# Out-projection put in the plan six matmuls at a time, with a later hand-over to TensorE assumed and one whole-bank group a chunk

## The chip, the cores and the metric

The kernel runs on one core of a Trainium2 chip. Its time is the device time of one execution in microseconds, as the median of several runs. Engines are named as in the profile: PE is TensorE (PEld its weight loads), DVE is VectorE, ACT is ScalarE, POOL is GpSimd, SP the queue that issues the transfers.

## The reference

A gated scan over 6080 steps of 256 features, and behind it two feed-forward layers from 256 to 2048 and back, the first with a leaky ReLU, the second with an ELU:

```python
for t in range(S):
    h = f[:, t] * h + i[:, t] * x[:, t]
    y[:, t] = h
...
h = x @ w_in
g = np.maximum(0.01 * h, h)                                        # first layer
g = np.where(h > 0.0, h, alpha * (np.exp(np.minimum(h, 0.0)) - 1.0))   # second layer
return (g @ w_out)
```

All is float32.

## The kernel before, in words

**Tiles.** The steps are cut into 12 chunks: eleven of 512 and, as number 4, one of 448 (`sizes`). Features lie on partitions, steps along the columns. The 2048 hidden features are worked through in four groups q = 0 to 3 of 512. A float32 product is made of three matmuls (`mm3`, L605 to L607): each operand is split into a high part and a rest, and high x high, high x rest and rest x high are summed in a PSUM bank of 128 x 512. Where the moving operand has 512 columns, `mm3` cuts it into two halves of 256 and does three matmuls on each, unless its last argument `whole` is true; then it does three of 512 columns.

**One group of one chunk** (`group`, by layer l, chunk c and group q). The in-projection is done with seven products in place of eight (`product`, six matmuls of 256 columns each, three for either hidden half). They go to three banks: X, R and Y, where Y is the bank `seed`. Between them X is copied out four times by ScalarE: `z1` (L688) into Y, `z2` and `z4` (`snap`, L652) into SBUF. VectorE adds the bank R to z4 (`add`, L655), and only then may the next product on R run. So three chains go from TensorE to ScalarE or on to VectorE and back to TensorE inside each group: product X(S1,T1), snapshot z4, addition C22, product R(A22,T4); and product X(S1,T1), snapshot z4, product X(S4,B22); and the same with z2. Then come the activations (in layer two an exponential, L715 and L726, and VectorE's L717 and L728), a cast to the high part by ScalarE (L744, L838) and the rest by VectorE (L747, L841). These are the operands of the out-projection, which sums into two banks `yb[0]` and `yb[1]` over the four groups of a chunk. For two of the four groups the odd half of the out-projection is again done with seven products (`some`). All the rest is `straight` (L772): operations O0, O1, E0, E1 (odd or even half, j = 0 or 1), each with two outputs k, so twelve matmuls of 256 columns. In the last operation of a group, E1, `whole` is set for q < 2 in layer one and q < 3 in layer two, and it is then six matmuls of 512 columns; the text calls such six a whole group. The last chunk of layer two is done with operands swapped (L785 to L787). In the short chunk all matmuls of the out-projection have 448 columns and are never cut.

**The order.** Nothing is ordered at run time. The program first collects all operations with an engine, an estimated cost, what each follows, and which buffer it takes and gives back (`Plan.add`). `Plan.emit` then plays a list schedule through with these costs: for the engine that can start soonest it takes, among the operations that can start within 0.1 of the first, the one with the earliest rank, which is handed back from the due times of those that use its result. An operation's result counts as ready for a user at its end, plus `late` (0.1 for TensorE), plus `HOP`, 0.15. From TensorE to TensorE nothing is added. The order in which operations are taken is the order of the instructions on each engine; the chip then runs each engine's row in that order and waits with semaphores.

Of the kernel before, what the change touches and what calls it, by code (L numbers as in the profile page):

```python
# [16 lines left out]
P = 128  # L17
# [9 lines left out]
class Plan:  # L27
# [3 lines left out]


    HOP = 0.15

    def __init__(self, pools):
        self.pools = {name: [(0.0, i, t) for i, t in enumerate(tiles)] for name, tiles in pools.items()}
# [2 lines left out]
    def add(self, engine, cost, due, run, after=(), take=(), give=(), late=0.0):  # L39
# [4 lines left out]
        self.ops.append(op)  # L44
        return op

    def emit(self, near):
        free = {}
        open_ = {}
        for i, op in enumerate(self.ops):  # L50
            op.index = i
            op.missing = len(op.after)
            for a in op.after:
                a.users.append(op)
            if not op.missing:
                open_.setdefault(op.engine, []).append(op)
        for op in reversed(self.ops):
            for u in op.users:
                t = u.rank - op.cost - op.late - self.HOP
                op.rank = t if op.rank is None else min(t, op.rank)  # L60
        left = len(self.ops)
        while left:
            best = None
            for e, ops in open_.items():
                starts = []
                for op in ops:
                    t = max(free.get(e, 0.0), op.ready)
                    want = {}
                    for _, _, pool in op.take:
                        want[pool] = want.get(pool, 0) + 1  # L70
                    for pool, n in want.items():
                        have = self.pools[pool]
                        t = max(t, heapq.nsmallest(n, have)[-1][0]) if len(have) >= n else float("inf")
                    starts.append((t, op))
                if not starts:
                    continue
                first = min(t for t, _ in starts)
                if first == float("inf"):
                    continue
                t, op = min(((t, op) for t, op in starts if t <= first + near), key=lambda p: (p[1].rank, p[1].index))  # L80
                if best is None or t < best[0]:
                    best = (t, op)
            if not best:
                for o in [o for v in open_.values() for o in v][:40]:
                    print(o.engine, o.run, [(p, len(self.pools[p])) for _, _, p in o.take])
            assert best, "no operation can start"
            t, op = best
            for store, name, pool in op.take:
                store[name] = heapq.heappop(self.pools[pool])
            end = t + op.cost  # L90
            free[op.engine] = end
            done = end + op.late + self.HOP
            op.run()
            for store, name, pool in op.give:
                _, i, tl = store[name]
                heapq.heappush(self.pools[pool], (done, i, tl))
            open_[op.engine].remove(op)
            for u in op.users:
                u.missing -= 1
                u.ready = max(u.ready, end if u.engine == op.engine == "PE" else done)  # L100
                if not u.missing:
                    open_.setdefault(u.engine, []).append(u)
            left -= 1
# [3 lines left out]
def kernel(  # L107
# [27 lines left out]
    KD = D // P  # L135
# [116 lines left out]
    for l, c, q in stream:  # L252
        n = sizes[c]
# [169 lines left out]
    def wop(u, s):  # L423

        return tuple(w[u][:, j * size[u] + s * P : j * size[u] + (s + 1) * P] for j in (0, 1))
# [188 lines left out]
    def group(i):  # L614
        l, c, q = stream[i]
        n = sizes[c]
# [3 lines left out]
        b = {}  # L620
# [112 lines left out]
        def gate(name, j):  # L733
            return b[name][2][:, j * 2 * CH : j * 2 * CH + 2 * n]

        gates = {}
# [33 lines left out]
            prev[0] = o  # L770

        def straight(name, r, j):  # L772
            def run(fresh):
                hi, lo = (gate(name, s)[:, j * n : (j + 1) * n] for s in (0, 1))
                if not swapped:
                    for k in range(KD):
                        mm3(yb[k][2][:, :n], wop((r, q), 2 * j + k), (hi, lo), k in fresh, False,
                            (r, j) == ("E", 1) and q < (2 if l == 1 else 3))
                    return

                wh, wl = (w[r, q][:, z * size[r, q] + j * D : z * size[r, q] + (j + 1) * D] for z in (0, 1))
                for t in range(n // P):
                    dst = yb[t // 2][2][:, t % 2 * D : (t % 2 + 1) * D]
                    ah, al = (s[:, t * P : (t + 1) * P] for s in (hi, lo))
                    nc.tensor.matmul(dst, ah, wh, start=t // 2 in fresh and t % 2 == 0, stop=False, skip_group_check=True)  # L785
                    nc.tensor.matmul(dst, ah, wl, start=False, stop=False, skip_group_check=True)  # L786
                    nc.tensor.matmul(dst, al, wh, start=False, stop=False, skip_group_check=True)  # L787

            out_(3 * KD, run, (0, 1), [gates[name], *wo[r]], [(b, name, "op")] if j else [])


        C11, C12, C21, C22 = (1, 1), (1, 0), (0, 1), (0, 0)
# [213 lines left out]
```

## Time and profile before

| | |
|---|---|
| Median of 3 runs | 1012.66 us (1011.34 to 1013.00) |
| The profiled execution | 1012.59 us, of which 1010.8 are its span |
| Mean granted clock of TensorE | 0.999 of full |
| VectorE, ScalarE busy | 883.9 us (87%), 775.4 us (77%) |
| The chain that ended last | 92% of the span on TensorE, 4% on VectorE, 2% on ScalarE |

The page gives the busy time of each engine and where the chain runs that ended last. A matmul is recorded as longer than the distance to the next one, since they overlap; how fast the stream goes is read from the starts in the timeline, with the number of rows between two of them.

### The profile page before, as it was taken

What the parts mean: (1) busy time and instruction counts of PE and PEld (TensorE: products, weight loads), DVE (VectorE), ACT (ScalarE), POOL (GpSimd) and SP (SyncE); (2) the same over time, 40 slices, a digit from 0 to 9 for tenths busy, and PEclk for the clock granted to TensorE, in tenths of its full rate; (3) what the DMA queues carried; (4) which work ended last, traced back from release to release, by engine and by line L of the source; (5) the groups of instructions that cost most, each with busy time, mean ns of one, the idle gap of its engine ahead of it and who ended that gap; (6) DMA issues with size and microseconds to landing.
All of it is one profiled execution on the core that took longest, in us unless ns stands there. A gap on an engine that the chain in (4) does not pass through costs nothing.

```text
span 1010.8 us, 19956 instructions
## 1 busy us (share of the span) xinstructions
PE 996.8 (99%) x8152; PEld 977.3 (97%) x8152; DVE 883.9 (87%) x1352; ACT 775.4 (77%) x1135; POOL 32.0 (3%) x38
## 2 busy tenths in 40 slices
PE   7999999999999999999999999999999999999998
PEld 6999999999999999999999999999999999999997
DVE  6899979999999999876688998998989989889875
ACT  6777777788887978876778877787877777877764
POOL 1120000011010000000000000000000000000000
PEclk9999999999999999999999999999999999999999
DMA  6542304345255443303840111101101021010110
GB/s 187 136 118 51 79 11 95 108 120 152 89 137 147 114 121 114 82 22 115 298 162 21 22 30 32 22 21 43 19 22 21 23 43 21 22 22 23 32 21 22
DMA packets 159083, 74.34 MB, mean 74 GB/s; under 512 B 132496, under 2 KB 146832, under 8 KB 158992
## 3 DMA queue, kind: packets, MB, share of 16 engines
q1 hardware_dynamic: 158992, 73.08, 27.0%
q8 instruction: 63, 1.03, 0.4%
q14 instruction: 28, 0.23, 0.1%
HBM read 48.01 MB, written 25.03 MB: 72 GB/s over the span
## 4 chain that ended last, share of the span: by engine, by line
PE 92%; DVE 4%; ACT 2%; DMA 1%; issue 1%; SPq 0%; DVEq 0%
PE bank L607 28%; PE bank L606 28%; PE bank L605 28%; PE seed L607 2%; PE seed L605 2%; PE seed L606 2%; DVE op L747 1%; PE bank L787 1%; DMA raw<-in_f_logit_dram 1%; PE bank L785 0%; ACT op L744 0%; PE bank L786 0%; DVE h L826 0%; DVE ws L717 0%; DVE op L841 0%
## 5 line engine op out<-in xcount | busy, mean ns | idle before, releaser
L605 PE MATMUL bank<-op,wI 128*128 128x256 f32 (+1 forms) x1152 | 321.5, 279 | 0.5 <-ACT sn L652 0.5
L607 PE MATMUL bank<-op,wI 128*128 128x256 f32 (+1 forms) x1152 | 320.7, 278 | 0.6 <-DVE wI L386 0.6
L606 PE MATMUL bank<-op,wI 128*128 128x256 f32 (+1 forms) x1152 | 320.7, 278 | 0.0
L606 PEld LDWEIGHTS bank<-op,wI 128*128 128x128 f32 x1152 | 218.6, 190 | 2.8 <-DVE op L492 0.2
L605 PEld LDWEIGHTS bank<-op,wI 128*128 128x128 f32 x1152 | 217.3, 189 | 3.6 <-ACT sn L652 0.7
L607 PEld LDWEIGHTS bank<-op,wI 128*128 128x128 f32 x1152 | 217.3, 189 | 0.9 <-DVE wI L386 0.9
L606 PE MATMUL bank<-op,wO 128*128 128x256 f32 (+2 forms) x680 | 190.6, 280 | 1.9 <-DVE op L747 1.6
L605 PE MATMUL bank<-op,wO 128*128 128x256 f32 (+2 forms) x680 | 190.4, 280 | 0.0
L607 PE MATMUL bank<-op,wO 128*128 128x256 f32 (+2 forms) x680 | 190.3, 280 | 0.0
L606 PE MATMUL bank<-op,wE 128*128 128x256 f32 (+2 forms) x600 | 182.0, 303 | 0.2 <-DVE op L747 0.2
L607 PE MATMUL bank<-op,wE 128*128 128x256 f32 (+2 forms) x600 | 181.8, 303 | 0.0
L605 PE MATMUL bank<-op,wE 128*128 128x256 f32 (+2 forms) x600 | 181.8, 303 | 0.0
L655 DVE TENSOR_TENSOR h<-bank,sn 128x512 f32<-128x512 f32 (+1 forms) x176 | 119.4, 678 | 26.4 <-ACT sn L652 13.9
L652 ACT COPY sn<-bank 128x512 f32<-128x512 f32 (+1 forms) x176 | 102.2, 580 | 43.0 <-PE bank L607 40.9
L606 PEld LDWEIGHTS bank<-op,wO 128*128 128x128 f32 x680 | 128.7, 189 | 2.5 <-DVE op L747 1.8
L607 PEld LDWEIGHTS bank<-op,wO 128*128 128x128 f32 x680 | 127.9, 188 | 0.2
L605 PEld LDWEIGHTS bank<-op,wO 128*128 128x128 f32 x680 | 127.8, 188 | 0.2
L607 PEld LDWEIGHTS bank<-op,wE 128*128 128x128 f32 x600 | 112.8, 188 | 4.9
L606 PEld LDWEIGHTS bank<-op,wE 128*128 128x128 f32 x600 | 113.5, 189 | 3.0 <-DVE op L747 0.4
L605 PEld LDWEIGHTS bank<-op,wE 128*128 128x128 f32 x600 | 112.8, 188 | 2.6
L747 DVE TENSOR_TENSOR op<-h,op 128x1024 fp32r<-128x1024 f32 (+1 forms) x78 | 96.5, 1237 | 17.8 <-ACT op L744 17.4
L747 DVE TENSOR_TENSOR op<-ws,op 128x1024 fp32r<-128x1024 f32 (+1 forms) x74 | 89.4, 1211 | 15.9 <-ACT op L744 15.9
(109 smaller groups left out, 1821.2 us busy)
## 6 DMA issues: line engine op xcount, KB each, us to landing
ws<-in_moe_w_in_dram SPq DMA_DIRECT2D x32, 255.6 KB, 3.6
ws<-in_moe_w_out_dram SPq DMA_DIRECT2D x32, 255.6 KB, 3.2
w2dI<-ws SPq DMA_DIRECT2D x16, 448.0 KB, 3.3
wI<-w2dI SPq DMA_DIRECT2D x8, 896.0 KB, 6.6
y1d<-t SPq DMA_DIRECT2D x22, 256.0 KB, 2.1
bt<-y1d SPq DMA_DIRECT2D x22, 256.0 KB, 2.8
out_dram<-t SPq DMA_DIRECT2D x80, 64.0 KB, 2.0
raw<-in_f_logit_dram SPq DMA_DIRECT2D x72, 64.0 KB, 3.3
```

The costliest lines, as they stand in the source:

```text
L605: nc.tensor.matmul(ps[:, s], wop[0], a[0][:, s], start=start and z == 0, stop=False, skip_group_check=True)
L606: nc.tensor.matmul(ps[:, s], wop[0], a[1][:, s], start=False, stop=False, skip_group_check=True)
L607: nc.tensor.matmul(ps[:, s], wop[1], a[0][:, s], start=False, stop=stop, skip_group_check=True)
L652: return act(s1(2 * h), None, lambda: nc.scalar.copy(out=ps(name), in_=ps("X")), after, take=[(b, name, "sn")])
L655: return dve(v1(2 * h), None, lambda: nc.vector.tensor_tensor(out=half(name, s), in0=two(ps(bank)), in1=two(ps(sn)), op=ALU.add), after, **k)
L747: gates[name] = dve(v1(2 * n), None, lambda name=name, g=g: nc.vector.tensor_tensor(out=gate(name, 1), in0=whole(g), in1=gate(name, 0).bit ...
L787: nc.tensor.matmul(dst, al, wh, start=False, stop=False, skip_group_check=True)
```

## The change

Three things are changed. A result of VectorE or ScalarE counts as ready for TensorE 0.35 after its end, 0.15 as before for any other user (`hop`, used in the ranks and in the readiness). The operations of `straight` are put into the plan one output k at a time, six matmuls each, so that other work may stand between them and each output bank is done for itself. And `whole` is left only in E1 of q = 0, which alone stays one operation over both outputs; E1 of q = 1, and of q = 2 in layer two, is now cut into halves.

```diff
+    SPARE = 0.2
...
+    def hop(self, op, user=None):
+        spare = op.engine in ("DVE", "ACT") and (user is None or user.engine == "PE")
+        return self.HOP + (self.SPARE if spare else 0.0)
...
-                t = u.rank - op.cost - op.late - self.HOP
+                t = u.rank - op.cost - op.late - self.hop(op, u)
...
+            later = end + op.late + self.hop(op)
...
-                u.ready = max(u.ready, end if u.engine == op.engine == "PE" else done)
+                u.ready = max(u.ready, end if u.engine == op.engine == "PE" else later if u.engine == "PE" else done)
...
         def straight(name, r, j):
+            def ops(s):
+                return gate(name, s)[:, j * n : (j + 1) * n]
+
+            unbroken = (r, j) == ("E", 1) and q < 1
+
+            def some_of(*ks):
+                def run(fresh):
+                    for k in ks:
+                        mm3(yb[k][2][:, :n], wop((r, q), 2 * j + k), (ops(0), ops(1)), k in fresh, False, unbroken)
+
+                return run
+
             def run(fresh):
-                hi, lo = (gate(name, s)[:, j * n : (j + 1) * n] for s in (0, 1))
-                if not swapped:
-                    for k in range(KD):
-                        mm3(yb[k][2][:, :n], wop((r, q), 2 * j + k), (hi, lo), k in fresh, False,
-                            (r, j) == ("E", 1) and q < (2 if l == 1 else 3))
-                    return
...
-            out_(3 * KD, run, (0, 1), [gates[name], *wo[r]], [(b, name, "op")] if j else [])
+            if swapped:
+                out_(3 * KD, run, (0, 1), [gates[name], *wo[r]], [(b, name, "op")] if j else [])
+                return
+            for ks in [tuple(range(KD))] if unbroken else [(k,) for k in range(KD)]:
+                out_(3 * len(ks), some_of(*ks), ks, [gates[name], *wo[r]], [(b, name, "op")] if j and ks[-1] == KD - 1 else [])
```

Line numbers of the changed kernel are higher: L605 to L607 become L611 to L613, L652 L658, L655 L661, L717 L723, L728 L734, L744 L750, L747 L753.

**VectorE, layer two, chunk 1, q = 3.** The last rows up to and around the addition that the product R(A22,T4) waits for (L655, now L661; `bt` and `op` with L455 or L461 are the operands of a later chunk). Before:

```order
L747 TENSOR_TENSOR op_128<-ws_135,op_128 128x1024
L455 TENSOR_TENSOR op_126<-bt_129,op_126 128x768
L728 SCALAR_TENSOR_TENSOR ws_136<-ws_136,h_130 128x1024
L455 TENSOR_TENSOR op_125<-bt_129,op_125 128x768
L747 TENSOR_TENSOR op_127<-ws_136,op_127 128x1024
L455 TENSOR_TENSOR op_125<-bt_129,op_125 128x256
L655 TENSOR_TENSOR h_132<-bank_116,sn_138 128x2x256
```

Now:

```order
L753 TENSOR_TENSOR op_122<-ws_134,op_122 128x1024
L461 TENSOR_TENSOR op_125<-bt_129,op_125 128x768
L461 TENSOR_TENSOR op_123<-bt_129,op_123 128x768
L734 SCALAR_TENSOR_TENSOR ws_135<-ws_135,h_132 128x1024
L661 TENSOR_TENSOR h_133<-bank_119,sn_138 128x2x256
L461 TENSOR_TENSOR op_123<-bt_129,op_123 128x256
L753 TENSOR_TENSOR op_126<-ws_135,op_126 128x1024
```

The small L455 and the wide L747 ahead of the addition have moved behind it, and L734, the counterpart of L728, stands directly in front.

**TensorE, layer two, chunk 1, E1 of q = 1.** `wE_74` is the weight of this operation. Before, and the first matmul of what follows:

```order
L605 MATMUL bank_115<-op_127,wE_74 128x512
L606 MATMUL bank_115<-op_127,wE_74 128x512
L607 MATMUL bank_115<-op_127,wE_74 128x512
L605 MATMUL bank_121<-op_127,wE_74 128x512
L606 MATMUL bank_121<-op_127,wE_74 128x512
L607 MATMUL bank_121<-op_127,wE_74 128x512
L605 MATMUL bank_120<-op_123,wI_69 128x256
```

Now:

```order
L611 MATMUL bank_118<-op_126,wE_74 128x256
L612 MATMUL bank_118<-op_126,wE_74 128x256
L613 MATMUL bank_118<-op_126,wE_74 128x256
L611 MATMUL bank_118<-op_126,wE_74 128x256
L612 MATMUL bank_118<-op_126,wE_74 128x256
L613 MATMUL bank_118<-op_126,wE_74 128x256
L611 MATMUL bank_116<-op_127,wI_69 128x256
```

The whole group has become two operations of six halves, and the first matmul of a product (`wI`) follows behind the one; the other six stand twelve rows further on.

**ScalarE, layer one, chunk 2, q = 2.** From the snapshot z1 (L688, now L694) over z2 to z4 (both L652, now L658). Before:

```order
L688 COPY seed_114<-bank_116 128x512
L299 CAST wI_69<-h_133 128x384
L299 CAST wI_70<-h_131 128x384
L299 CAST wI_69<-h_133 128x128
L652 COPY sn_137<-bank_116 128x512
L299 CAST wI_70<-h_131 128x128
L701 ACTIVATE h_132<-seed_114 128x2x256
L652 COPY sn_138<-bank_116 128x512
```

Now:

```order
L694 COPY seed_114<-bank_116 128x512
L712 ACTIVATE h_131<-h_131 128x1024
L658 COPY sn_137<-bank_116 128x512
L305 CAST wI_69<-h_133 128x384
L305 CAST wI_70<-h_130 128x384
L305 CAST wI_69<-h_133 128x128
L305 CAST wI_70<-h_130 128x128
L750 CAST op_124<-h_131 128x1024
L658 COPY sn_138<-bank_116 128x512
```

All four casts of weights (L305) and the wide cast of an operand (L750) now stand between z2 and z4; before, three of the four and the wide one stood ahead of z2. In TensorE's row, six matmuls now stand between the product that z4 copies and the next on that bank, where it was twelve.

## Rows read from the trace of the kernel before

**Rows 1.** The page, section 1 (engines) and the granted clock in 40 slices.

```profile
PE 996.8 (99%) x8152; PEld 977.3 (97%) x8152; DVE 883.9 (87%) x1352; ACT 775.4 (77%) x1135; POOL 32.0 (3%) x38
...
PEclk9999999999999999999999999999999999999999
```

**Rows 2.** TensorE's timeline from 374 us: start us, us, engine line op.

```profile
373.89 0.28 PE L605 MATMUL bank<-op,wI 128*128 128x256 f32 x1
...
395.99 0.28 PE L605 MATMUL seed<-op,wI 128*128 128x256 f32 x1
```

**Rows 3.** Timeline of TensorE, 753 to 768 us, first and last row.

```profile
752.80 0.28 PE L605 MATMUL bank<-op,wO 128*128 128x256 f32 x1
...
768.00 0.28 PE L605 MATMUL bank<-op,wE 128*128 128x256 f32 x1
```

**Rows 4.** Windows of TensorE: us, busy (matmuls), clock, DMA share, GB/s.

```profile
299.00:325.00 26.00, 26.00 (x222) 1.00 0.37 109
582.00:667.00 85.00, 85.00 (x689) 1.00 0.14 31
746.00:973.00 227.00, 227.00 (x1837) 1.00 0.12 25
```

**Rows 5.** TensorE's timeline at 560 us, a wait in q=1.

```profile
560.39 0.31 PE L605 MATMUL bank<-op,wI 128*128 128x256 f32 x1
560.53 0.28 PE L606 MATMUL bank<-op,wI 128*128 128x256 f32 x1
560.65 0.28 PE L607 MATMUL bank<-op,wI 128*128 128x256 f32 x1
```

**Rows 6.** TensorE's timeline at 745 us, a wait in q=3.

```profile
745.68 0.35 PE L605 MATMUL bank<-op,wI 128*128 128x256 f32 x1
745.88 0.28 PE L606 MATMUL bank<-op,wI 128*128 128x256 f32 x1
```

**Rows 7.** Timeline of TensorE, 524 to 526 us, around a whole group.

```profile
524.63 0.40 PE L605 MATMUL bank<-op,wE 128*128 128x512 f32 x1
...
526.03 0.28 PE L605 MATMUL bank<-op,wI 128*128 128x256 f32 x1
...
526.38 0.28 PE L605 MATMUL bank<-op,wI 128*128 128x256 f32 x1
```

**Rows 8.** Timeline of TensorE, 750 to 752 us, around another whole group.

```profile
750.70 0.39 PE L605 MATMUL bank<-op,wE 128*128 128x512 f32 x1
...
752.10 0.28 PE L605 MATMUL bank<-op,wI 128*128 128x256 f32 x1
```

**Rows 9.** Groups by form: whole-bank matmuls of one line (others alike).

```profile
L606 PE MATMUL bank<-op,wE 128*128 128x512 f32 x104 | 41.1, 395 | 0.0
```

**Rows 10.** VectorE's timeline, 743 to 746 us, before that wait.

```profile
743.44 1.22 DVE L747 TENSOR_TENSOR op<-ws,op 128x1024 fp32r<-128x1024 f32 x1 [0.63 <-ACT op L744]
744.58 0.42 DVE L455 TENSOR_TENSOR op<-bt,op 128x256 fp32r<-128x256 f32 x1
744.92 0.68 DVE L655 TENSOR_TENSOR h<-bank,sn 128x512 f32<-128x512 f32 x1
```

**Rows 11.** VectorE's timeline, 552 to 560 us, before a wait in q=1.

```profile
552.45 0.69 DVE L717 SCALAR_TENSOR_TENSOR ws<-ws,seed 128x512 f32<-128x512 f32 x1 [0.35 <-ACT ws L715]
...
559.58 0.68 DVE L655 TENSOR_TENSOR h<-bank,sn 128x512 f32<-128x512 f32 x1
```

**Rows 12.** Timeline of TensorE, 719 to 725 us, the entry to chunk 5.

```profile
720.79 0.38 PE L605 MATMUL bank<-op,wI 128*128 128x256 f32 x1 [0.52 <-ACT sn L652]
```

**Rows 13.** ScalarE groups by form: busy us, mean ns, idle before.

```profile
L652 ACT COPY sn<-bank 128x512 f32<-128x512 f32 x160 | 93.7, 585 | 39.8 <-PE bank L607 38.0
...
L299 ACT CAST wI<-h 128x384 fp32r<-128x384 f32 x8 | 3.8, 509 | 1.8 <-DVE h L273 1.8
...
L299 ACT CAST wI<-h 128x128 fp32r<-128x128 f32 x8 | 2.2, 297 | 0.4 <-DVE h L273 0.4
...
L744 ACT CAST op<-h 128x1024 fp32r<-128x1024 f32 x72 | 75.6, 1050 | 0.9
```

More of the change, by code (lines that the diff above doesn't have):

```diff
@@ L783, in run @@
                     dst = yb[t // 2][2][:, t % 2 * D : (t % 2 + 1) * D]
-                    ah, al = (s[:, t * P : (t + 1) * P] for s in (hi, lo))
+                    ah, al = (ops(s)[:, t * P : (t + 1) * P] for s in (0, 1))
                     nc.tensor.matmul(dst, ah, wh, start=t // 2 in fresh and t % 2 == 0, stop=False, skip_group_check=True)
```

## The prediction

> **What bounds the kernel now.** I read the page first: TensorE is busy for 99% of the span, at full clock in all forty slices, 2.4 GHz, so a busy share says nothing more [rows 1]. What is left to see is how far apart its matmuls start, and that is in the timeline of TensorE alone. Between 373.89 and 395.99 us, 195 steps of 256 columns take 22.10 us: 113.3 ns each [rows 2]. Between 752.80 and 768.00 us, 129 steps of the same size take 15.20 us: 117.8 ns [rows 3]. The stream has two paces, 4.5 ns apart, and the granted clock is 1.00 in the slow stretches too, so the clock is not what separates them [rows 4].
>
> What changes the pace is seen next. At 560.39 and at 745.68 us a product on bank R, which must wait for VectorE's addition (L655), starts its second matmul 0.14 and 0.20 us later instead of 0.113, and the steps behind it are 0.12 [rows 5, 6]. A wait of 0.03 to 0.08 us thus costs little itself, but leaves the stream slow. At 524.63 a group of six whole-bank matmuls comes by, and behind it the steps are 0.113 again [rows 7]; at 750.70 another comes by and the stream stays slow [rows 8, 3]. Following every wait over 0.03 us through the timeline, I count 14 stretches behind one: 6 were fast at once, 6 slow until the next whole group, 2 slow until something large broke them (582 to 667 and 746 to 973 us). These two hold most of the loss.
>
> **The change, part by part.** The sum is made against the profiled execution, 1012.59 us, which is the median of the runs shown (1012.66) less 0.07.
>
> *The long slow stretches.* Both begin at the same place, the addition in group q = 3 of a layer-two chunk. VectorE idles 0.63 us for ScalarE's cast, does L747 and a small L455, then the addition, 744.92 to 745.60, and the matmul that needs it stands at 745.68 [rows 6, 10]. In the changed order L747 and that L455 stand behind the addition, and L734 (L728 of before) stands in front. Counting from the start of product X(S1,T1): the snapshot of X ends at 1.57, since ScalarE comes to it 0.1 late; L734 waits for an exponential that ends at 0.58, and ends at 1.83; the addition then runs from 1.76 to 2.44 (durations and overlaps as in [rows 10]). The product on R stands 24 matmuls from that start, as before, 24 x 0.1133 = 2.72. That leaves 0.28 us, where before 0.08 was left between its end and the matmul's late start. I take the wait as gone in all ten full chunks. In the two windows there are 689 + 1837 = 2526 matmuls, 132 of them whole, so some 2390 at 4.5 ns, 10.7 us [rows 4]. The third wait of this kind, at 541 us, cost 42 steps, 0.2 us, and the waits themselves 3 x 0.08. Together **-11.1 us**; 0 if the wait stays.
>
> *The wait in q = 1 of layer two.* Here nothing is won: from L717, which waits for an exponential, VectorE works without a break up to the addition, 552.45 to 559.58 [rows 11], and both orders put the same VectorE work and the same 87 matmuls between the product that starts this chain and the one that ends it. Before, this wait came in three chunks only, since a slow stream has no need to wait; with a fast one it comes in each of ten. It costs 0.035 us [rows 5] and 30 slow steps up to the chunk's whole group, 0.14: seven more, **+1.2 us**. Ends: -0.5 (none left) and the price of staying slow, a rival below.
>
> *Whole banks.* 104 x 3 = 312 whole matmuls are 52 groups of six [rows 9]; one a full chunk leaves 21, so 31 go. Six whole ones take 1.40 us, 233 ns each, fast or slow [rows 7, 8]; two halves at the fast pace take 226.7. So 31 x 6 x 6.7 ns = **-1.2 us**; at the slow pace two halves take 235.6, which would make it +0.4. The Trainium skill (TensorE: Matmul & The Clock Gate, "Wait — 56ns, not 53.3ns?") has each matmul cost its columns at 2.4 GHz and a fixed 2.5 ns more. By it 186 more matmuls would cost +0.5 us, and the sum would be 1.7 us higher; the rows measure the wide one as the dearer.
>
> *The entry to chunk 5 of layer two.* After the short chunk TensorE stands idle 0.52 us for a snapshot [rows 12], and twice more before 724 us. Split operations put 77.25 matmuls (of 256 columns) over this chain instead of 72: 5.25 x 0.1133 = **-0.6 us** (0 to -1.2, if the waits behind it shrink as much again).
>
> *New waits in layer one.* The new order takes cover away in two places. In chunk 2, q = 2, product X(S4,B22) now follows X(S1,T1) with 6 matmuls between, 12 before, and ScalarE has the four casts L305 and the wide L750 between the two snapshots. From the end of X(S2,T2) ScalarE needs 0.58 + 2 x 0.51 + 2 x 0.30 + 1.05 + 0.58 = 3.8 us [rows 13], less five overlaps of some 0.08 as in [rows 10], and 0.3 to start and to hand over; TensorE has 30 x 0.1133 = 3.4. A wait of 0.3 us follows, more if VectorE is late with what is cast. In chunk 7, q = 2, a wide cast moves in the same way between the snapshots: 0 to 0.6. Behind each the stream may be slow for some 325 steps, as the next whole group is a chunk away, 1.5 us. Against that, the slow steps from 299 to 325 us, 222 of them, 1.0 us [rows 4], may or may not come back. I take 0.6 for the waits and 1.4 for the pace, **+2.0 us** (-1.0 to +3.6).
>
> DMA issues, GpSimd and the operand stages move by a few places, and the list of TensorE's waits has none on a load after the first 20 us: at nothing, since the loads land long before their use; a load that came late would show as a wait of TensorE in tenths. The last chunk keeps its operations whole and its order: nothing.
>
> Sum: 1012.6 - 11.1 + 1.2 - 1.2 - 0.6 + 2.0 = **1002.9 us**.
>
> **The rivals.** (1) *One stretch stays slow.* Of 14 waits, 2 left a pace that whole groups did not break. If the wait at chunk 5 does so, layer two stays slow from 724 to 973 us, some 2130 steps, 9.6 us, less six waits of q = 1: 1011.5. If the one at chunk 7 of layer one does, 323 to 667 us are slow, 13.1 us less 2.2: 1013.8. For it: there is no later wait to shake it loose. Against: 12 of 14. (2) *The wait in q = 3 stays*, because ScalarE reaches the snapshot 0.3 us later than I worked out: then the long stretches come as before, 1012.6 - 1.2 - 0.6 + 2.0 = 1012.8. For it: ScalarE works without a break there. The change would then do nothing that it says. (3) *Slower.* The one mechanism: with 31 whole groups gone and the small waits too, nothing breaks a slow pace once it has come. If the stream turns slow for good at chunk 7 of layer one, and again behind the short chunk, 323 to 973 us are slow: 1002.9 + 10.9 + 8.6 = 1022.4. It decides at the first whole group behind 323 us: if the steps behind it are 0.118, this is the case. For it is that the whole group at 750.70 broke nothing [rows 8]; against it, the groups at 34, 325, 524, 546, 564 and 727 us did. (4) *Better.* No new wait and none in q = 1: 998.
>
> **How the numbers follow.** A measurement of this kernel tells 0.2%, 2 us, from no change: faster is below 1010.6, slower above 1014.7. I give my forecast 0.66 (998 to 1008), the better case 0.04, one slow stretch 0.12, the wait in q = 3 0.08, slow for good 0.10. The first two are faster, 0.70; the next two are the same, 0.20; the last slower, 0.10. The range goes from the better case, 998, to 1012.5, which takes in about half of the two middle cases.
>
> **What would show it.** Right: steps of 0.113 us in 582 to 667 and 746 to 973 us, no wait at the addition of q = 3, and a short slow stretch of 30 steps in q = 1 of each layer-two chunk. The whole groups number 21. New waits near 127 and 323 us. Wrong: steps of 0.118 over tens of microseconds behind any wait; or a wait of over 0.03 us at the addition of q = 3, where L734 would end later than 1.83 us behind the product's start.

## The result, and the profile after

| | before | after |
|---|---|---|
| Median (lowest to highest, runs) | 1021.49 us (1011.34 to 1024.93, 19) | 1006.29 us (999.79 to 1011.36, 19) |
| The profiled execution, its span | 1012.59 us, 1010.8 | 1008.28 us, 1006.3 |

The ratio of the times is 0.9894, 95% interval 0.9869 to 0.9919: faster by 1.1%; the two medians alone lie 1.5% apart. (Ratios here leave out runs more than 1.5% above the fastest of their kernel.) Both kernels spread by over ten microseconds from one execution to the next, and the three runs of before that were shown ahead of the prediction were at the low end. The two profiled executions are therefore only 4.3 us apart, and none of the slower executions of before has a profile: what its median of 1021.49 consists of is not shown. The changed kernel was profiled twice more, among the experiments, at 1002.53 and 1001.90 us.

The page of after, engines and granted clock, against [rows 1]:

```profile
PE 992.5 (99%) x8338; PEld 980.5 (97%) x8338; DVE 876.7 (87%) x1352; ACT 773.5 (77%) x1135; POOL 37.1 (4%) x38
...
PEclk9999999999999999999999999999999999999999
```

TensorE is still the bound, at the same clock. The timeline of TensorE, first and last row of a stretch behind 733 us and of one behind 569 us:

```profile
733.24 0.28 PE L611 MATMUL seed<-op,wI 128*128 128x256 f32 x1
...
755.00 0.28 PE L611 MATMUL bank<-op,wE 128*128 128x256 f32 x1
...
569.82 0.28 PE L612 MATMUL bank<-op,wI 128*128 128x256 f32 x1
...
591.96 0.28 PE L611 MATMUL bank<-op,wE 128*128 128x256 f32 x1
```

The first has 192 steps in 21.76 us, 113.3 ns each; the second 188 in 22.14 us, 117.8 ns. The two paces of [rows 2, 3] are there unchanged; what changed is where they lie. From 746 to 973 us, slow before [rows 4], the stream is now fast; from 531 to 669 us it is slow. The windows view (us, busy and matmuls, clock, DMA share, GB/s) shows the same clock in both:

```profile
531.00:669.00 138.00, 138.00 (x1156) 1.00 0.11 24
733.00:968.00 235.00, 235.00 (x2042) 1.00 0.12 25
```

The addition of q = 3 in layer two, chunk 5, in VectorE's timeline, and the start of the next product in TensorE's, against [rows 6, 10]:

```profile
745.73 1.23 DVE L734 SCALAR_TENSOR_TENSOR ws<-ws,h 128x1024 f32<-128x1024 f32 x1
746.88 0.69 DVE L661 TENSOR_TENSOR h<-bank,sn 128x512 f32<-128x512 f32 x1
747.48 0.41 DVE L461 TENSOR_TENSOR op<-bt,op 128x256 fp32r<-128x256 f32 x1
...
747.86 0.28 PE L611 MATMUL bank<-op,wI 128*128 128x256 f32 x1
```

The addition ends at 747.57, 0.29 us ahead of that product; the wait is gone. The one in q = 1 is still there, at the same place of the chunk as in [rows 5]:

```profile
767.92 0.31 PE L611 MATMUL bank<-op,wI 128*128 128x256 f32 x1
768.06 0.28 PE L612 MATMUL bank<-op,wI 128*128 128x256 f32 x1
768.18 0.28 PE L613 MATMUL bank<-op,wI 128*128 128x256 f32 x1
```

It is 0.14 in place of 0.113 long, and the stream is fast again five steps behind it. The entry to chunk 5 and the two new waits of layer one, chunk 2 and chunk 7, each in q = 2:

```profile
727.50 0.39 PE L611 MATMUL bank<-op,wI 128*128 128x256 f32 x1 [0.23 <-DVE h L661]
...
130.71 0.38 PE L611 MATMUL bank<-op,wI 128*128 128x256 f32 x1
...
329.68 0.39 PE L611 MATMUL bank<-op,wI 128*128 128x256 f32 x1 [0.38 <-ACT sn L658]
```

And the groups by form, against [rows 9]: 42 whole matmuls a line, which is 21 groups of six.

```profile
L612 PE MATMUL bank<-op,wE 128*128 128x512 f32 x42 | 16.6, 395 | 0.0
```

**Where the time went.** Counting every step of TensorE from the starts in the two traces, where a step of 256 columns of 116 to 121 ns is a slow one and a longer one a step that waited: 3101 slow steps before, 2132 after, 13.6 and 9.3 us over the fast pace, so -4.3. Steps that waited, behind the first 25 us, cost 6.4 and 7.5 us, +1.0, and ahead of that +0.2. The whole matmuls cost 1.8 and 0.7 us more than halves, -1.1; what comes after the last matmul has started, -0.2. That is -4.4 of the 4.5 by which the spans differ. In the two later profiles of the changed kernel there are 1234 and 1055 slow steps. Their spans are 5.8 and 6.5 us shorter than that of the first, of which slow steps are 4.0 and 4.8 and shorter waits the rest. The same count can be made in every trace of the experiments below: the span, less what slow steps, steps that waited and whole or otherwise cut matmuls cost above the fast pace, is 984.9 to 986.3 us in all fourteen, whose spans go from 999.8 to 1024.6. So slow steps and waits account for the differences between these kernels, whatever sets the pace.

**What holds a slow stretch.** The one from 531 us begins behind a wait of 0.05 us for ScalarE's snapshot in layer two, chunk 0, and three whole groups pass without ending it. One that began at 412 us was ended by the next group. TensorE's timeline at the wait, at a group that did nothing, and at one that released:

```profile
532.14 0.38 PE L611 MATMUL bank<-op,wI 128*128 128x256 f32 x1
532.37 0.28 PE L612 MATMUL bank<-op,wI 128*128 128x256 f32 x1
...
567.96 0.39 PE L611 MATMUL bank<-op,wE 128*128 128x512 f32 x1
568.18 0.39 PE L612 MATMUL bank<-op,wE 128*128 128x512 f32 x1
568.41 0.40 PE L613 MATMUL bank<-op,wE 128*128 128x512 f32 x1
...
449.57 0.40 PE L611 MATMUL bank<-op,wE 128*128 128x512 f32 x1
449.81 0.40 PE L612 MATMUL bank<-op,wE 128*128 128x512 f32 x1
450.04 0.39 PE L613 MATMUL bank<-op,wE 128*128 128x512 f32 x1
```

The distances of the whole ones differ: 0.22 and 0.23 us at the start of the group without effect, 0.24 and 0.23 in the one that released (in nanoseconds mostly 231, 229, 236 or 230, 230, 235 there, 236, 236, 231 or 233, 233, 234 here). The first two distances add up to 459 to 461 ns in every group of six, in all the traces, that met a slow stream and left it slow, and to 466 to 473 in every one that released it. So there are at least two slow paces, equal in speed, which a whole matmul tells apart. Below they are called the loose and the stuck one.

### The profile page after: what moved, and what is told of

Same layout as the page of the kernel before. It is cut to its first block, busy times and chain, and to the rows that moved or that the text cites. A ratio compares the mean times of both kernels' runs of the same rounds, so it can differ in the third digit from the quotient of the medians.

```text
span 1006.3 us, 20314 instructions
## 1 busy us (share of the span) xinstructions
PE 992.5 (99%) x8338; PEld 980.5 (97%) x8338; DVE 876.7 (87%) x1352; ACT 773.5 (77%) x1135; POOL 37.1 (4%) x38
## 4 chain that ended last, share of the span: by engine, by line
PE 92%; DVE 4%; ACT 1%; issue 1%; DMA 1%; SPq 0%; DVEq 0%
PE bank L611 28%; PE bank L613 28%; PE bank L612 28%; PE seed L613 2%; PE seed L612 2%; PE seed L611 2%; DMA raw<-in_f_logit_dram 1%; PE bank L799 1%; PE bank L797 0%; PE bank L798 0%; DVE bt L579 0%; DVE op L753 0%; DVE h L661 0%; DVE ws L378 0%; ACT op L750 0%
## 5 line engine op out<-in xcount | busy, mean ns | idle before, releaser
L611 PE MATMUL bank<-op,wI 128*128 128x256 f32 (+1 forms) x1152 | 321.0, 279 | 0.6 <-ACT sn L658 0.4
L613 PE MATMUL bank<-op,wI 128*128 128x256 f32 (+1 forms) x1152 | 320.1, 278 | 0.7 <-DVE wI L392 0.7
L611 PEld LDWEIGHTS bank<-op,wI 128*128 128x128 f32 x1152 | 217.4, 189 | 3.1 <-DVE h L661 0.8
L613 PEld LDWEIGHTS bank<-op,wI 128*128 128x128 f32 x1152 | 217.3, 189 | 1.2 <-DVE wI L392 1.2
L612 PE MATMUL bank<-op,wE 128*128 128x256 f32 (+2 forms) x662 | 191.5, 289 | 0.0
L611 PE MATMUL bank<-op,wE 128*128 128x256 f32 (+2 forms) x662 | 191.5, 289 | 0.0
L613 PE MATMUL bank<-op,wE 128*128 128x256 f32 (+2 forms) x662 | 191.3, 289 | 0.0
L611 PE MATMUL bank<-op,wO 128*128 128x256 f32 (+2 forms) x680 | 190.1, 280 | 0.0
L613 PE MATMUL bank<-op,wO 128*128 128x256 f32 (+2 forms) x680 | 189.8, 279 | 0.0
L661 DVE TENSOR_TENSOR h<-bank,sn 128x512 f32<-128x512 f32 (+1 forms) x176 | 119.3, 678 | 46.8 <-PE bank L613 34.2
L658 ACT COPY sn<-bank 128x512 f32<-128x512 f32 (+1 forms) x176 | 102.2, 581 | 35.1 <-PE bank L613 33.5
L613 PEld LDWEIGHTS bank<-op,wO 128*128 128x128 f32 x680 | 127.9, 188 | 0.2
L611 PEld LDWEIGHTS bank<-op,wO 128*128 128x128 f32 x680 | 127.9, 188 | 0.1
L613 PEld LDWEIGHTS bank<-op,wE 128*128 128x128 f32 x662 | 124.5, 188 | 2.2
L612 PEld LDWEIGHTS bank<-op,wE 128*128 128x128 f32 x662 | 124.8, 188 | 1.0
L611 PEld LDWEIGHTS bank<-op,wE 128*128 128x128 f32 x662 | 124.5, 188 | 1.2
L753 DVE TENSOR_TENSOR op<-h,op 128x1024 fp32r<-128x1024 f32 (+1 forms) x78 | 96.0, 1231 | 10.3 <-ACT op L750 9.9
L753 DVE TENSOR_TENSOR op<-ws,op 128x1024 fp32r<-128x1024 f32 (+1 forms) x74 | 88.4, 1209 | 17.2 <-ACT op L750 17.2
```

Of the source, the lines that this page charges most:

```text
L611: nc.tensor.matmul(ps[:, s], wop[0], a[0][:, s], start=start and z == 0, stop=False, skip_group_check=True)
L612: nc.tensor.matmul(ps[:, s], wop[0], a[1][:, s], start=False, stop=False, skip_group_check=True)
L613: nc.tensor.matmul(ps[:, s], wop[1], a[0][:, s], start=False, stop=stop, skip_group_check=True)
L658: return act(s1(2 * h), None, lambda: nc.scalar.copy(out=ps(name), in_=ps("X")), after, take=[(b, name, "sn")])
L661: return dve(v1(2 * h), None, lambda: nc.vector.tensor_tensor(out=half(name, s), in0=two(ps(bank)), in1=two(ps(sn)), op=ALU.add), after, **k)
L753: gates[name] = dve(v1(2 * n), None, lambda name=name, g=g: nc.vector.tensor_tensor(out=gate(name, 1), in0=whole(g), in1=gate(name, 0).bit ...
```

## The experiments

**Theory A**: the time is the number of slow steps and of real waits; the order decides where waits come, a wait may turn the pace slow, and whole groups turn it back. **Rival B**: the pace comes and goes by itself, and the gain is narrow matmuls and less waiting. All medians below are to be held against kernels of the same session: before had 1014.95 us in the first (24 runs, 1009.30 to 1023.60), 1014.34 in the second (35, 1003.46 to 1021.65), and 1011.17 in the third (16, 1004.19 to 1021.10).

### One part of the change at a time

*The later hand-over alone.*

```diff
+    SPARE = 0.2
...
+                u.ready = max(u.ready, end if u.engine == op.engine == "PE" else later if u.engine == "PE" else done)
```

> The kernel before with the later hand-over (0.35 in place of 0.15 for TensorE's users) and nothing else: operations of twelve matmuls, whole groups for q < 2 and q < 3, 52 of them. Theory A (two paces of TensorE's stream, 113.3 and 117.8 ns a step; waits on VectorE's addition set it slow, and the later hand-over takes those waits out of the plan): the waits in q = 3 of layer two are gone or fewer, and the time is 5 to 15 us below the kernel before, some 1005 to 1014 us. Rival B (the gain comes from the split operations and from narrow matmuls in place of whole ones, and the paces come and go without regard to the plan): within 2 us of the kernel before, some 1020 us. Rival C (an operation of twelve can't be fitted into the gap, so that the hand-over moves waits without removing them): waits at other places, 1015 to 1022 us.

Measured: 1023.60 us (1018.43 to 1028.32, 7 runs), ratio 1.0098 (1.0063 to 1.0133). Slower than all three numbers; waits at other places, as in rival C, but far larger than it had them. One part of Theory A came true all the same: no addition in q = 3 of layer two is waited for any more. The list of waits of its profile, its TensorE in layer two, and ScalarE ahead of that:

```profile
PE bank L611 <- ACT sn L658: 11.3, 18, 0.9
```

```profile
774.17 0.39 PE L611 MATMUL bank<-op,wI 128*128 128x256 f32 x1 [0.24 <-ACT sn L658]
...
775.70 0.39 PE L612 MATMUL bank<-op,wO 128*128 128x256 f32 x1 [0.45 <-DVE op L847]
```

```profile
771.87 0.82 ACT L844 CAST op<-ws 128x768 fp32r<-128x768 f32 x1
772.60 1.05 ACT L844 CAST op<-h 128x1024 fp32r<-128x1024 f32 x1
773.54 0.57 ACT L658 COPY sn<-bank 128x512 f32<-128x512 f32 x1
```

TensorE waits 11.3 us in all for snapshots, 18 times; before, the list has 0.5 us for one. The snapshot stands behind two wide casts, which ScalarE does without a break, and TensorE's row has nothing left to put in between. The same comes back in each full chunk of layer two: steps of 0.5 to 0.7 and of 0.7 to 1.2 us in place of 0.113. The slow steps are fewer than before (2145, 9.4 us), but waits cost 24.5 us in place of 6.4. That operations of twelve are what leaves the row without filling is argued from the next runs, not shown by this one.

*The split alone.*

```diff
-    SPARE = 0.2
+    SPARE = 0.0
...
-            unbroken = (r, j) == ("E", 1) and q < 1
+            unbroken = (r, j) == ("E", 1) and q < (2 if l == 1 else 3)
```

> The changed kernel with the hand-over of before (0.15 for all) and the whole groups of before; only the operations of the out-projection are put in the plan six matmuls at a time. Theory A: the plan again takes a result of VectorE as ready early, so the waits at the additions stay, and the long slow stretches with them: within 5 us of the kernel before, 1015 to 1025 us. Rival B (the split is what gains): 1006 to 1010 us, at most 4 us above the changed kernel.

Measured: 1006.20 us (1001.58 to 1017.67, 7 runs), ratio 0.9907 (0.9870 to 0.9944). Rival B's number, against Theory A as it was put: operations of six gain by themselves what the whole change gains. The addition in q = 3 of layer two is not waited for either; it has 0.31 us to spare in chunks 5 to 10. In its layer two behind 738 us TensorE waits 0.05 us a chunk for a snapshot, 0.08 for a rest (L753) and 0.02 for an addition. But the pace is not beside the point: the execution profiled is the slowest of the seven, 1017.67 us, and was slow from 34 to 184 us and from 291 to 678, 4635 slow steps in all, 20.3 us. Its whole groups met the stuck pace, 22 of them from 295 us on, and released nothing.

*Whole groups in q = 0 alone, old order.*

```diff
-                            (r, j) == ("E", 1) and q < (2 if l == 1 else 3))
+                            (r, j) == ("E", 1) and q < 1)
```

> The kernel before, with every operation in its old place, and whole matmuls in q = 0 alone: 21 whole groups in place of 52, the other 31 cut into halves. Theory A (a whole group releases the slow pace): the waits stay and there are fewer groups to release them, so 0 to 8 us slower than before, 1021 to 1029 us, with slow stretches that end at the groups of q = 0. Rival B (two halves are 6.7 ns dearer than... in place of it: a whole matmul is 6.7 ns dearer than two halves, and that is all): 31 x 6 x 6.7 ns = 1.2 us faster than before, 1020 us.

Measured: 1018.72 us (1010.41 to 1025.77, 12 runs), ratio 1.0045 (1.0012 to 1.0077). Slower where their price alone says 1.2 us faster: rival B falls here, and the time is in Theory A's 0 to 8 us. The profiled execution has 5570 slow steps, 24.4 us; slow from 280 to 676 and from 734 to 983 us. But these stretches did not end at the groups of q = 0, as Theory A had it: all 16 groups in them met the stuck pace and released nothing. So by which step fewer whole groups cost time in the old order is not shown.

*No whole group, new order.*

```diff
-                        mm3(yb[k][2][:, :n], wop((r, q), 2 * j + k), (ops(0), ops(1)), k in fresh, False, unbroken)
+                        mm3(yb[k][2][:, :n], wop((r, q), 2 * j + k), (ops(0), ops(1)), k in fresh, False)
```

> The changed kernel with every operation in its place and no whole matmul at all: its 21 whole groups are cut into halves too. Theory A (a whole group releases the slow pace): with nothing to release it, the stream stays slow from an early wait on for hundreds of microseconds, 5 to 20 us above the changed kernel, 1011 to 1026 us; the slow stretches that ended at 123 and 449 us run on. Rival B (a whole matmul is only dearer, the pace comes back by itself): 21 x 6 x 6.7 ns = 0.8 us below the changed kernel, 1005.5 us.

Measured: 1015.71 us (1006.38 to 1023.74, 12 runs), ratio 0.9994 (0.9961 to 1.0028): the gain is gone. The windows of its profile (us, busy and matmuls, clock, DMA share, GB/s):

```profile
238.00:675.00 437.00, 437.00 (x3712) 1.00 0.33 94
734.00:974.00 240.00, 240.00 (x2118) 1.00 0.13 26
```

437 / 3712 is 117.7 ns a matmul, 240 / 2118 is 113.3. One wait of 0.03 us, at 238 us, turns the stream slow, and nothing turns it back for 437 us. From 734 us on it is fast to the end of the chunks, past five waits of 0.03 us. A wait can leave either pace, and in this execution, without a whole group, the pace stayed.

### Pairs, and the change again

*The change without the hand-over; the change with the whole groups of before; the change with the whole groups of before in threes; the change itself.*

```diff
-    SPARE = 0.2
+    SPARE = 0.0
```

> The changed kernel with the hand-over of before: split operations and whole groups in q = 0 alone. Theory A2 (the split is the part that gains; the hand-over is worth little on top; fewer whole groups release less): 1003 to 1012 us, between the changed kernel and 6 us over it. Rival C2 (hand-over and split only work together, and the split alone was fast by luck of its 52 whole groups): over 1012 us.

```diff
-            unbroken = (r, j) == ("E", 1) and q < 1
+            unbroken = (r, j) == ("E", 1) and q < (2 if l == 1 else 3)
```

> The changed kernel with whole groups as before (q < 2 in layer one, q < 3 in layer two, one operation over both outputs each): split operations and the later hand-over. Theory A2: whole groups are worth more as releases than the 1.2 us that they cost, so at or below the changed kernel, 999 to 1006 us. Rival D2 (a whole group as one operation of 6 x 233 = 1.4 us is too long for the later hand-over, as in the run with the hand-over alone): new waits of TensorE of tenths of a us in each chunk of layer two, 1010 to 1020 us.

```diff
-                        mm3(yb[k][2][:, :n], wop((r, q), 2 * j + k), (ops(0), ops(1)), k in fresh, False, unbroken)
+                        mm3(yb[k][2][:, :n], wop((r, q), 2 * j + k), (ops(0), ops(1)), k in fresh, False,
+                            (r, j) == ("E", 1) and q < (2 if l == 1 else 3))
```

> The changed kernel with every operation in its place, but whole matmuls also in E1 of q = 1, and of q = 2 in layer two, as before; there they come as three and three, with other work between. After the first runs: the split gained without the hand-over, the hand-over alone lost, and without whole groups the changed order is 9 us slower. Theory A2 (any whole matmuls release the slow pace, now and then, so more of them release it sooner): 31 x 1.2/31 us dearer, +1.2, and up to 6 us of slow steps less: 1000 to 1006 us, at or below the changed kernel. Rival B2 (a group of three doesn't release, six do): the changed kernel + 1.2 us, 1006 to 1009 us.

> The changed kernel itself once more, on the chip of the three others, so that they can be held against it. All theories: 1000 to 1011 us, median 1006 us, ratio to before 0.987 to 0.994.

| hand-over | split | whole in q = 0 alone | median us (range, runs) | ratio to before |
|---|---|---|---|---|
| | yes | yes | 1008.49 (1001.72 to 1016.13, 12) | 0.9984 (0.9950 to 1.0018) |
| yes | yes | | 1011.41 (1009.13 to 1014.14, 12) | 1.0022 (0.9995 to 1.0048) |
| yes | yes | whole as before, new order | 1006.53 (1002.07 to 1012.45, 12) | 0.9955 (0.9917 to 0.9992) |
| yes | yes | yes (the change) | 1002.64 (999.59 to 1013.53, 12) | 0.9936 (0.9900 to 0.9972) |

The first is where Theory A2 had it, the second where rival D2 had it (Theory A2 fails there), and the change is faster again, inside the range expected. With the split and one whole group a chunk in place the hand-over is worth 5.9 us (1008.49 to 1002.64), where by itself it cost 8.7 (1023.60 to 1014.95). With hand-over and split, one whole group a chunk is worth 8.8 us (1011.41 to 1002.64), where in the old order it cost 3.8 (1018.72 to 1014.95). But each of the two pays only beside the split and beside the other: the split alone has 0.9907 (0.9870 to 0.9944), and with only one of them added 1.0022 or 0.9984, intervals that lie above it, though from another session. With both it is 0.9936 here and 0.9894 in the other two sessions. That the change gains anything over the split alone is therefore not shown; they were not run in one session. Hand-over and fewer whole groups without the split weren't tried.

Why the whole groups of before cost 8.8 us beside the other two is seen in TensorE's timeline of that kernel, layer two:

```profile
807.05 0.39 PE L612 MATMUL bank<-op,wO 128*128 128x256 f32 x1
...
808.31 0.39 PE L611 MATMUL bank<-op,wI 128*128 128x256 f32 x1
...
809.38 0.38 PE L611 MATMUL bank<-op,wI 128*128 128x256 f32 x1
```

In each full chunk three steps are long, by 0.1, 0.23 and 0.27 us, for VectorE's rest (L857), a snapshot and an addition; waits cost 14.5 us in all, against 4.9 in the change profiled beside it, with about as many slow steps (1457 and 1234). That is rival D2, and the picture of the hand-over alone, smaller. Whole operations of 1.4 us go together with those waits; the order that the plan makes around them is another one, so which of its places does it is open.

The whole groups of before in the new order cost 3.9 us more than the change by the medians, with intervals that overlap, and showed something else. Timeline of TensorE, layer two, around two groups of three:

```profile
775.81 0.28 PE L613 MATMUL bank<-op,wI 128*128 128x256 f32 x1
...
776.49 0.28 PE L613 MATMUL bank<-op,wE 128*128 128x256 f32 x1
776.60 0.39 PE L611 MATMUL bank<-op,wE 128*128 128x512 f32 x1
...
777.30 0.28 PE L611 MATMUL bank<-op,wI 128*128 128x256 f32 x1
...
778.59 0.28 PE L613 MATMUL bank<-op,wI 128*128 128x256 f32 x1
```

Six steps take 0.68 us ahead of the group, 113 ns; behind it eleven take 1.29, 117 ns. The next group of three makes the stream fast again. The time is the one of rival B2, but its reason fails: three whole matmuls do release, and as surely turn fast into slow.

### Other cuts

*By turns other cuts of a bank in E1 of q = 1 to 3, first output.*

```diff
-        parts = [slice(0, n)] if n < CH or whole else [slice(0, HC), slice(HC, CH)]
+        at = whole if whole > 1 else HC
+        parts = [slice(0, n)] if n < CH or whole is True else [slice(0, at), slice(at, CH)]
...
+                        at = (448, 384, 320, 288, 272, 480, True)[(3 * (c + 11 * l) + q) % 7] if (r, j, k) == ("E", 1, 0) and q else 0
```

> The changed kernel, with the first output (k = 0) of E1 in q = 1, 2 and 3 cut in other ways than 256 + 256: by turns 448 + 64, 384 + 128, 320 + 192, 288 + 224, 272 + 240, 480 + 32 and 512 whole, some nine times each. The time says little (0 to 6 us above the changed kernel); the question is what each cut does to the pace. What the runs so far show: three whole matmuls turn fast into slow and slow into fast, six leave fast as it is and release some slow stretches, and the 448-column matmuls of the short chunk were fast behind every time. Theory A3 (the pace is how the steps fall against a beat of the machine, and what counts is the length of the odd piece): some cut, 448 + 64 if any, leaves fast as fast and makes slow fast, nine times of nine. Rival B3 (only whole matmuls touch the pace): pace before and behind a cut is the same for all but the whole one. Rival C3 (any odd piece throws the dice): either pace behind any cut, whatever it was before.

One execution, 1017.98 us (before 1008.91 beside it). Pace ahead of and behind every group of wide matmuls in the fourteen traces of this case, outside the short chunks and what lies next to them (for 512 columns from all kernels; the cuts from this one and the two below):

| group | fast ahead | slow ahead |
|---|---|---|
| six of 512 | 216 of 216 stay fast | loose: 45 of 45 fast behind; stuck: 89 of 89 stay slow |
| three of 512 | 14 of 14 slow behind | stuck: 20 of 20 fast; loose: 3 of 4 fast |
| 384 + 128 | 5 of 5 stay fast | 3 of 3 fast |
| 320 + 192 | 20 of 20 stay fast | 5 of 7 fast |
| 448 + 64 | 7 of 7 stay fast | 0 of 2 fast |
| 288 + 224 | 6 of 6 slow behind | 0 of 1 fast |
| 272 + 240 | 3 of 3 slow behind | 5 of 5 fast |
| 480 + 32 | 6 of 6 slow behind | 2 of 3 fast |

Behind a fast stream each form of group gave the same pace every time: rival C3, the dice, falls there, and rival B3 too. Behind a slow one three rows go both ways. In the row of three whole ones the loose cases differ in their distances again (the first two add up to 466 or 467 ns in the three that released, to 472 in the one that did not), so there may be more than two slow paces; for the cuts nothing here tells the kinds apart. Theory A3 has its cut in 384 + 128, in the eight groups counted, not in 448 + 64. A release in TensorE's timeline of this kernel:

```profile
880.83 0.28 PE L614 MATMUL bank<-op,wI 128*128 128x256 f32 x1
...
881.54 0.28 PE L614 MATMUL seed<-op,wI 128*128 128x256 f32 x1
881.65 0.34 PE L612 MATMUL bank<-op,wE 128*128 128x384 f32 x1
...
882.17 0.22 PE L612 MATMUL bank<-op,wE 128*128 128x128 f32 x1
...
882.74 0.28 PE L614 MATMUL bank<-op,wE 128*128 128x256 f32 x1
...
883.53 0.28 PE L612 MATMUL bank<-op,wI 128*128 128x256 f32 x1
```

Six steps in 0.71 us ahead, 118 ns; seven in 0.79 behind, 113 ns. The cut itself costs: ten steps from its first on take 1.31 us in place of 1.13, and with 320 + 192 1.23.

*320 + 192 in place of the whole group; three whole ones and 320 + 192; the change beside them.*

```diff
-                        mm3(yb[k][2][:, :n], wop((r, q), 2 * j + k), (ops(0), ops(1)), k in fresh, False, unbroken)
+                        mm3(yb[k][2][:, :n], wop((r, q), 2 * j + k), (ops(0), ops(1)), k in fresh, False, "cut" if unbroken and k == 0 else False)
```

> The changed kernel with no whole matmul; in their place the first output of E1 in q = 0 is cut 320 + 192 and the second into halves, every operation in its place. In the survey of cuts the ten steps from a 320 + 192 on took 1.23 us in place of 1.13 and all seven were fast behind, one of them slow ahead of it; the 21 whole groups cost 21 x 6 x 6.7 ns = 0.8 us. Theory A3 (320 + 192 releases any slow pace and leaves a fast one alone): + 21 x 0.10 - 0.8 = +1.3 us, and no slow stretch runs past a chunk's cut, which leaves some 3 us of slow steps where the changed kernel had 5 to 9: 999 to 1004 us, with less spread. Rival B3 (only whole matmuls release, the one 320 + 192 was chance): as without whole groups, 1012 to 1018 us. Rival C3 (it releases one kind of slow stretch and not the one that a wait leaves behind): 1004 to 1010 us.

```diff
+                        mm3(yb[k][2][:, :n], wop((r, q), 2 * j + k), (ops(0), ops(1)), k in fresh, False, ("cut" if k else True) if unbroken else False)
```

> The same, with three whole matmuls on the first output and 320 + 192 on the second. Three whole ones turn a stuck slow pace fast, a fast one slow, and release the slow pace of which six release; a 320 + 192 behind them would then make all three fast. Cost against the changed kernel: 21 x 0.10 - 0.4 = +1.7 us. Theory A3: 999.5 to 1004.5 us, 0.4 above the run with 320 + 192 alone. Rival C3 (320 + 192 needs the whole ones ahead of it): below the run with 320 + 192 alone, 999 to 1004 us to its 1004 to 1010. Rival B3 (it leaves the pace as it is): the three whole ones turn each fast stretch slow until the next group, half of all steps are slow, 3700 x 4.5 ns = 17 us: 1010 us or more.

> The changed kernel on the same chip, to hold the two against. All theories: median 1002 to 1007 us, between 999 and 1014.

Measured: 1003.99 us (1002.75 to 1006.66, 10 runs), ratio 0.9924 (0.9886 to 0.9961); 1003.25 us (1002.12 to 1005.47, 7 runs), 0.9916 (0.9874 to 0.9958); the change 1002.21 us (1001.50 to 1003.38, 6 runs), 0.9894 (0.9854 to 0.9934). Behind three whole ones and 320 + 192 the stream was fast 20 times of 20, as Theory A3 had it, with 708 slow steps in the profile, the fewest of all. 320 + 192 alone let two stretches pass, which is rival C3's mechanism and against Theory A3, at a time on the border of both. In the profile of the pair the cuts cost 2.4 us, against 0.5 saved on 63 whole matmuls and 1.5 on 347 fewer slow steps than in the change beside it, so their price takes the gain back. Neither beats the changed kernel.

## Why the prediction was right

The time came out faster, as forecast, and in the range. The forecast 1002.9 us lies 3.4 below the median of the result and within 0.7 of the change's two later medians, 1002.64 and 1002.21. That it lies so close is partly luck: the sum starts from one execution of before, and such executions go from 1003.46 to 1024.93 us, so that the 2 us said to tell a change from none, taken from three runs, were far too few. The fastest of before is within 1.3 us of those medians of the change.

*The long slow stretches, -11.1.* The step on the wait was right: the spare time of the addition in q = 3 was put at 0.28 us and is 0.29, and behind 733 us the stream is fast in all three profiles of the change, but for 30 steps now and then. The reason is not the hand-over by itself, which alone is slower, nor L734 in front of the addition alone: the change without the hand-over (1008.49 us) has no wait at that addition either, nor has the split alone, with 0.31 us to spare, or the hand-over alone. So either part removes this wait, and only the split does it without larger ones elsewhere. In size the term is right only by the execution: slow steps fell by 1867 and 2046 in the two later profiles, 8.2 and 9.0 us (13.6 less 5.4 and 4.6), and by 969, 4.3 us, in the one that came with the result, because the stretch from 531 to 669 us is a stuck one.

*One stretch stays slow* was rival 1. It happened, at a place not named: not chunk 5 of layer two or chunk 7 of layer one, but behind the snapshot wait of 0.05 us in chunk 0. It cost some 1110 slow steps, 4.9 us, less than the rival's 8.6 to 10.9, since the short chunk ended it. "12 of 14" was the wrong sort of count: what decides is the kind of slow pace, and a stuck one is never released by six whole matmuls.

*The wait in q = 1, +1.2.* Right in the wait, 0.03 to 0.045 us a chunk; too dear in the pace. In the three profiles 4 of the 19 such waits that the stream met fast made it slow up to the whole group 3.4 us later, the others for some steps only. Ten waits and two such stretches are 0.4 + 0.3 = 0.7 us.

*Whole banks, -1.2.* As a price right: the two traces give -1.1. The Trainium skill (TensorE: Matmul & The Clock Gate, "Wait — 56ns, not 53.3ns?") has the columns at 2.4 GHz and 2.5 ns more, as an estimate 109.2 ns for 256 columns and 215.8 for 512; the runs show 113.3 or 117.8 and 233, so the measurement decides against it here, in both. What the term left out is that whole groups act on the pace too: they release the loose one, and the same 31 groups taken out of the old order made it 3.8 us slower, not 1.2 faster. Only the rival of a slow pace for good spoke of it, and the run without whole groups (1015.71) is its milder form.

*The entry to chunk 5, -0.6.* The steps that waited cost 1.5 us there before and 0.5 after: -1.0, inside the bounds of 0 to -1.2.

*New waits in layer one, +2.0.* Both came where they were expected. With the step behind each they cost 0.27 us in chunk 2 (0.3 expected) and 0.65 in chunk 7 (0 to 0.6). The pace behind them was fast in the profile of the result; in the third profile some 320 slow steps, 1.4 us, the price that was set, came in chunk 7 behind the next wait, for an addition 1.5 us later. But the list of new waits was not complete. The two largest others came where none was expected, for a rest of a weight (L392) at 81 us and for an addition in chunk 9, q = 2:

```profile
81.46 0.38 PE L613 MATMUL seed<-op,wI 128*128 128x256 f32 x1 [0.56 <-DVE wI L392]
...
412.37 0.38 PE L611 MATMUL bank<-op,wI 128*128 128x256 f32 x1
```

With the step behind each they cost 0.83 us (0.40 in the two later profiles), where it was 0.12 before, and 0.26; against that one of 0.50 at 256 us is gone. In the profile of the result each was followed by a slow stretch, of 353 and 315 steps. "At nothing" for the operand stages, argued from loads alone, was thus the term without a good reason. From 25 us to the start of layer two, waits and slow steps together cost 3.4 us more than before in that profile and 0.3 and 1.3 us more in the two later ones: all inside the bounds of -1.0 to +3.6, but in part from other places.

*Slower, rival 3*, did not come in the change, because the stuck pace is not the rule behind a wait, and whole groups end the loose one. Fewer whole groups in the old order showed its picture, slow from 280 to 676 and from 734 to 983 us in an execution of 1022.77 us.

## What to carry to other kernels

Where TensorE's busy share says nothing, count the distance of its starts: a wait of 0.03 us can cost a hundred times its length if the stream stays slower behind it. A knob of a planner and the size of its pieces have to be tried together: a later hand-over lost 8.7 us with pieces of twelve matmuls and won 5.9 with pieces of six, and that only where a single group a chunk was left whole. Try each part alone as well: the split by itself had as large a gain as was shown for the three together. And a single profiled execution of such a kernel may stand ten microseconds from the next, so hold medians of many runs of one session against each other.

## What the runs showed of the hardware that was not expected

The stream of matmuls keeps a state. At the granted clock of 1.00 it runs at 113.3 or at 117.8 ns per 256 columns, and stays so over hundreds of microseconds. A wait can change it, and so does a group of other widths, in a way that repeats: six of 512 columns keep fast and release one kind of slow (45 of 45) and never the other (0 of 89), and three of 512 exchange fast and the stuck slow (14 of 14 and 20 of 20). Slow paces that can't be told apart by 256-column steps differ in the distances of 512-column ones, 231, 229, 236 ns against 236, 236, 231 or 233, 233, 234. What in the engine keeps this state isn't settled by these runs: the traces show where matmuls start, not why.
